# An RWKV-6 recurrence with a feed-forward layer behind it: the v loads of twenty chunks requested by ScalarE's queue instead of SyncE's

## The chip, the cores and the metric

The kernel runs on one core of a Trainium2 chip. The metric is the device time of one execution in microseconds, the median of several runs. A core has five engines that work through a queue of instructions each: TensorE (PE in the profile; its weight loads are PEld), VectorE (DVE), ScalarE (ACT), GpSimd (POOL) and SyncE (SP). Data moves between the memory of the chip (HBM) and the core's on-chip memory by DMA: an engine issues a request, and 16 DMA engines carry it out while the engine goes on. SP computes nothing and does little else than issue requests.

## What is computed

Inputs r, k, v, w have 4 batches, 8 heads, 768 positions and 48 numbers per head, in float32. For each batch and head a 48 x 48 state is carried along the positions; then a feed-forward layer follows.

```
for t in range(S):
    cur = einsum('bhd,bhe->bhde', u * k[t], v[t])
    y[t] = einsum('bhd,bhde->bhe', r[t], state + cur)
    state = w[t][..., None] * state + einsum('bhd,bhe->bhde', k[t], v[t])
x = y as [3072, 384]
h = x @ w_in                 # 384 -> 2048
out = maximum(0.01 * h, h) @ w_out   # 2048 -> 384
```

## The kernel before, in words

**Tiles and stages.** The positions are cut into chunks of 128: 6 chunks for each of 4 batches, 24 in all. Chunks 0 to 3 are worked on two at a time (`pair`, line 487), chunks 4 to 23 are the twenty single chunks (`single`, line 694). For a single chunk:
- Four loads bring w, k, r and v of the chunk (192 KB each, in rows of 192 bytes) into the four quarters of one buffer of the pool "in", which has 11 buffers (lines 705 to 711). All four are requested by SP.
- ACT takes the logarithm of w (line 718), PE sums it along the positions (724), DVE adds (736), ACT takes exponentials (745, 750, 754), DVE multiplies them with r and k into rk (407), and rk is transposed, by PE with copies by ACT or DVE (418, 423, 425) or by a DMA (771).
- POOL casts v to bfloat16, vb (line 457), and makes the bonus term: k times u (437), times r (441), DVE's sum over the head (445), times v into vs (449). POOL also scales the state, sb (782).
- PE multiplies the scores (864), DVE masks them (795). PE then forms the sums k x v for the next state out of rk and vb (line 805), and the chunk's output out of sb (831) and of the masked scores and vb (836). Both need vb. DVE adds vs to the output (482), and it is transposed into xT (468 with 473 or 475, or 849).

The feed-forward layer takes one or two chunks at a time in 14 blocks: PE multiplies xT with w_in (line 1030), ACT applies the leaky maximum while it copies to g (1045), PE multiplies g with w_out (1060). The last seven blocks multiply with seven products instead of eight of the halves (line 960, with sums by DVE at 941 and copies by ACT at 976 and DVE at 981).

**What sets the order.** The kernel first writes down 1124 steps, each with its possible engines and what it depends on (`Plan.add`). The list ORDER (lines 100 to 153) is a fixed sequence of all steps, and FORCE names the engine of a step that has more than one. `Plan.order` walks along ORDER with a model of times: it keeps a clock for each engine, decides from it which buffer of a pool a step gets, and for a load holds the issuing engine back while more than 150 KB would be in flight. The instructions are then written out in ORDER, so every engine's queue is ORDER cut down to the steps of that engine; nothing is reordered on the chip. Real waits are by semaphores: an instruction waits until the data it reads has been written and the buffer it writes is no longer read. Modelled times also decide how many warm-up matmuls (line 1099) are put into PE's early gaps, for planned times under 24 us.

The steps of the twenty v loads are 148, 177, 206, 226, 266, 298, 330, 353, 390, 410, 450, 470, 507, 527, 562, 582, 619, 639, 670, 696, for chunks 4 to 23 in this order. In ORDER the v load stands where its turn in SP's queue comes, among steps of other engines that were planned later in time; for instance

```
... 780, 783, 224, 236, 241, 225, 235, 242, 243, 177, ...   (177: chunk 5's v load; 780: ACT, line 1045)
... 273, 285, 226, ...   (226: chunk 7's v load; 273: ACT, line 750)
... 1029, 639, ...   (639: chunk 21's v load; 1029: ACT, line 976)
```

Of the kernel before, what the change touches and what calls it, by code (L numbers as in the profile page):

```python
# [22 lines left out]
class Plan:  # L23
# [16 lines left out]
    def order(self, pools):  # L40
        left = [len(s[3]) for s in self.steps]
        users = [[] for _ in self.steps]
        for i, s in enumerate(self.steps):
            for j in s[3]:
                users[j].append(i)
        remain, free = {}, {p: [(0.0, k) for k in range(len(t))] for p, t in pools.items()}
        for s in self.steps:
            for b in (*s[4], *s[5]):
                remain[id(b)] = len(b.users)
        n = len(self.steps)  # L50
        self.start, self.done, self.eng, ready = [None] * n, [0.0] * n, [None] * n, [0.0] * n
        at, wire_free, landed, flying = dict(self.BEGIN), 0.0, 0.0, []
        for i in ORDER:
            engs, fn, deps, reads, takes, wire = self.steps[i][0], *self.steps[i][1:2], *self.steps[i][3:]
            if left[i]:
                raise RuntimeError(("before its inputs", i))
            e = FORCE.get(i) or next(iter(engs))
            now = max(at[e], ready[i])
            for b in takes:
                if b.t is None:  # L60
                    slot = min(free[b.pool])
                    free[b.pool].remove(slot)
                    now, b.slot, b.t = max(now, slot[0]), slot[1], pools[b.pool][slot[1]]
            touched = list({id(b): b for b in (*reads, *takes)}.values())
            for b in touched:
                if b.pool == "ps":
                    now = max([now, *(t for q, t in b.seen.items() if q != e)])
            self.start[i], self.eng[i] = now, e
            at[e] = now + engs[e] - (self.OVER[e] if engs[e] > 0.3 else 0.0)
            if wire is None:  # L70
                self.done[i] = now + engs[e] + self.SEEN[e]
            else:
                time, size, lat, lead = wire
                while flying and sum(x for _, x in flying) + size > 150:
                    at[e] = max(at[e], flying.pop(0)[0])
                wire_free = max(wire_free, at[e] + lead) + time
                flying.append((wire_free, size))
                landed = self.done[i] = max(wire_free + lat, landed + 0.7 * time)
            for b in touched:
                b.seen[e] = self.done[i]  # L80
                b.free_at = max(b.free_at, self.done[i])
                remain[id(b)] -= sum(u == i for u in b.users)
                if not remain[id(b)]:
                    free[b.pool].append((b.free_at, b.slot))
            for j in users[i]:
                left[j] -= 1
                ready[j] = max(ready[j], self.done[i])
        if len(set(ORDER)) != n or len(ORDER) != n:
            raise RuntimeError(("order", n, len(ORDER)))
        return ORDER  # L90


LOAD = (1.1, 64, 1.4, 0.2)
# [60 lines left out]
FORCE = {4: "ACT", 6: "DVE", 24: "ACT", 27: "ACT", 30: "DVE", 33: "ACT", 47: "ACT", 57: "ACT", 59: "DVE", 60:  # L154
    "ACT", 62: "DVE", 80: "ACT", 83: "ACT", 86: "DVE", 89: "ACT", 103: "ACT", 113: "DVE", 115: "DVE", 116:
    "DVE", 118: "DVE", 120: "POOL", 122: "POOL", 124: "POOL", 126: "POOL", 128: "ACT", 129: "POOL", 131: "ACT",
    132: "POOL", 134: "DVE", 135: "ACT", 137: "POOL", 138: "POOL", 140: "POOL", 141: "POOL", 143: "POOL", 144:
# [10 lines left out]
def kernel(  # L168
# [11 lines left out]
    nc = tc.nc  # L180
    B, H, S, D = r.shape
    L = 128
# [77 lines left out]
    with tc.manual_schedule():  # L260
# [10 lines left out]
        for t in pools["lw"]:  # L271
# [3 lines left out]
            out=trev[:], in_=trev[:], compare_op=ALU.is_ge, fill=0.0,  # L275
# [5 lines left out]
            out=tstr2[:], in_=tstr2[:], compare_op=ALU.is_gt, fill=0.0,  # L281
# [4 lines left out]
            out=ident[:], in_=ident[:], compare_op=ALU.is_equal, fill=0.0,  # L286
# [3 lines left out]
            out=maskb[:], in_=maskb[:], compare_op=ALU.is_gt, fill=0.0,  # L290
            base=0, pattern=[[1, 128]], channel_multiplier=-1,
        )
        for tile_, op in ((mask2, ALU.is_gt), (spread, ALU.is_equal)):
            for q in (0, 64):
                nc.gpsimd.affine_select(
                    out=tile_[q : q + 64, :, :], in_=tile_[q : q + 64, :, :], compare_op=op, fill=0.0,
# [58 lines left out]
        def columns(n):  # L355
            xb, off = place[n]
            return lambda: xb.t[:, :, off : off + L]
# [23 lines left out]
        for part in (1, 2):  # L381
            def rest(e, part=part):
# [8 lines left out]
                out=u_rows.t[0:1, :], in_=u_row.t[0:1, :]),  # L391
# [302 lines left out]
        def single(n):  # L694
            b, c = seq[n]
            t0 = c * L
            P0 = n * 10
            first, last = c == 0, c == C - 1
            rows[n] = out[b * S + t0 : b * S + t0 + L, :]
            slot = Buf("in")  # L700

            def part(i):
                return lambda: slot.t[:, i * DM : (i + 1) * DM].rearrange("p (h d) -> p h d", h=H)

            lds = []
            for i, src in enumerate((w, k, r, v)):
                def load(e, src=src, i=i):
                    nc.sync.dma_start(out=part(i)(), in_=src[b, :, t0 : t0 + L, :].rearrange("h p d -> p h d"))
                lds.append(step(
                    {"SP": 0.62}, load, P0 + i * 0.1, takes=[slot], wire=LOAD,  # L710
                    deps=[firsts[n - AHEAD]] if n - AHEAD in firsts else []))
            wl, kl, rl, vl = lds
            wv, kv, rv, vv = (part(i) for i in range(4))
# [5 lines left out]
                P0, deps=[wl], reads=[slot], takes=[lw])  # L719
# [3 lines left out]
            def cum(e):  # L723
# [13 lines left out]
                P0, deps=[s_cum], reads=[cp, lw], takes=[ci])  # L737
# [3 lines left out]
            for half in range(0 if first else 2):  # L741
# [4 lines left out]
                        out=a_in.t[q0 : q0 + 64, :, half], in_=cp.t[q0 : q0 + 64, DM : DM + NP], func=AF.Exp),  # L746
                    P0, deps=[s_cum], reads=[cp], takes=[a_in]))
# [3 lines left out]
                P0, deps=[s_cum, s_ci], reads=[cp])  # L751
# [3 lines left out]
                P0, deps=[s_ci], reads=[ci], takes=[ek])  # L755
# [3 lines left out]
                P0, deps=[rl, s_er], reads=[slot, cp], takes=[rk])  # L759
            s_k = step(  # L760
                {"DVE": 0.55}, lambda e: mult(rk.t[:, 1, :, 0:D], heads(ek.t), kv()),
                P0, deps=[kl, s_ek], reads=[slot, ek], takes=[rk])
# [5 lines left out]
            else:  # L768
# [3 lines left out]
                        out=rkT.t[:], in_=rk.t[:].rearrange("p a h d -> p (a h d)")),  # L772
                    P0, deps=[s_r, s_k], reads=[rk], takes=[rkT], wire=TRK)]
# [3 lines left out]
            if not first:  # L777
# [5 lines left out]
                        out=sb.t[:].rearrange("p g a d -> p (g a) d"),  # L783
# [12 lines left out]
                    out=m.t[:, par, :, :], in0=sc[par].t[:].rearrange("p (g t) -> p g t", g=NP),  # L796
# [49 lines left out]
            else:  # L846
# [3 lines left out]
                        out=columns(n)(), in_=y.t[:].rearrange("p h d -> p (h d)")),  # L850
# [4 lines left out]
        def run(ns):  # L855
            works = [single(n) for n in ns]
            asked = [next(x) for x in works]

            def scores(e):
                for sc, rkT, _ in asked:  # L860
                    for p in range(NP):
                        for par in range(2):
                            q0 = 64 * par
                            nc.tensor.matmul(  # L864
                                sc[par].t[:, p * 128 : (p + 1) * 128], lhsT=rkT.t[q0 : q0 + D, NP + p, :],
                                rhs=rkT.t[q0 : q0 + D, p, :], start=True, stop=True, skip_group_check=True)

            s_sc = step(
                {"PE": 0.19 + 0.231 * len(ns)}, scores, ns[-1] * 10 + 1, deps=[s for x in asked for s in x[2]],
                reads=[x[1] for x in asked], takes=[b for x in asked for b in x[0]])  # L870
            given.append(s_sc)
            for x in works:
                next(x, None)
# [142 lines left out]
        for nb, size in enumerate(blocks):  # L1016
# [7 lines left out]
            for j in range(0, NJ, J):  # L1024
# [15 lines left out]
                if j == 0:  # L1040
                    for ch in chs:
# [4 lines left out]
                        out=g.t[:, j : j + J, 0:N],  # L1046
                        in_=hp.t[:, 0 : J * N].rearrange("p (a n) -> p a n", a=J), func=AF.Prelu, alpha=0.01),
# [86 lines left out]
```

## Time and profile before

| | |
|---|---|
| runs before | 179.13 us median of 3 (179.12 to 180.2) |
| span of the profiled execution, first to last instruction | 177.0 us |
| median of the runs less this span | 2.1 us |
| ACT's DMA requests in the profile | 1 (u, 1.5 KB) |
| SP's loads of w, k, r, v for single chunks | 80, of 192 KB each |
| busy share of PE, DVE, ACT, POOL | 96, 81, 64, 61% |

The profile gives no time of its own for the profiled execution beside the span; 2.1 us is taken for what lies around it. A row of the timeline has the start in us, the length in us, the engine and line, what is written and read, how many instructions are merged into the row, and in brackets how long the engine sat idle before it and what ended that. Rows of a DMA request (SPq, ACTq) tell how long the issuing queue was held, not how long the data took. A row of the view by stretches has, after its bounds, its length and then the busy times of PE, PEld, DVE, ACT and POOL with the number of instructions, the granted clock, the DMA share and GB/s. A row of a line's view has its number of instructions with the shortest, median and longest duration in ns. A row of the waits has the total in us, the number of waits, and the longest.

### The profile page before, as it was taken

How to read it: one execution, taken by the hardware profiler on the slowest of the kernel's cores; microseconds unless marked ns; L12 is line 12 of the kernel's file. 1: busy time of each engine (PE TensorE's matmuls, PEld its weight loads, DVE VectorE, ACT ScalarE, POOL GpSimd, SP SyncE). 2: the span in 40 equal slices, each digit the busy share in tenths (PEclk: the TensorE clock that was granted, in tenths of full speed). 3: DMA queues.
4: the chain of work that ended last, by engine and by line, in shares of the span. 5: the costliest groups of instructions: out<-in, count | busy, mean ns of one | idle time of the engine just before them, and what ended most of it. 6: DMA issues, size and time to landing. Idle time of an engine off the chain costs nothing.

```text
span 177.0 us, 5530 instructions
## 1 busy us (share of the span) xinstructions
PE 170.4 (96%) x2155; PEld 139.9 (79%) x2158; DVE 143.5 (81%) x299; ACT 114.0 (64%) x263; POOL 107.3 (61%) x143
## 2 busy tenths in 40 slices
PE   7999999999999999999999999999999998999993
PEld 2566779867768877777779899899899997799992
DVE  7498935267599899889879999999999999956662
ACT  5676769734677794796379964676769950178500
POOL 5989946486749859879599093391693959100000
PEclk9999999999999999999999999999999999999999
DMA  5999999999999999999999999996999897432104
GB/s 138 261 271 340 350 300 195 351 231 199 201 206 195 191 199 227 163 201 179 198 206 195 197 208 209 163 222 124 210 194 196 188 226 78 118 101 80 44 26 157
DMA packets 115885, 34.25 MB, mean 194 GB/s; under 512 B 108305, under 2 KB 115090, under 8 KB 115858
## 3 DMA queue, kind: packets, MB, share of 16 engines
q1 hardware_dynamic: 115856, 33.89, 93.1%
q8 instruction: 17, 0.28, 0.7%
q14 instruction: 10, 0.08, 0.2%
q10 hardware_dynamic: 2, 0.00, 0.0%
HBM read 25.17 MB, written 4.72 MB: 169 GB/s over the span
## 4 chain that ended last, share of the span: by engine, by line
PE 69%; DVE 15%; ACT 5%; issue 4%; DMA 3%; POOL 2%; DVEq 0%; SPq 0%; ACTq 0%
PE ps L1030 30%; PE ps L1060 13%; PE ps L960 10%; DVE rk L407 3%; DMA rkT<-rk 3%; PE ps L864 3%; DVE in L941 2%; PE ps L418 2%; ACT g L425 2%; PE ps L724 1%; PE ps L836 1%; DVE ci L736 1%; PE ps L518 1%; DVE dg L445 1%; ACT ps L750 1%
## 5 line engine op out<-in xcount | busy, mean ns | idle before, releaser
L1030 PE MATMUL ps<-xT,w_in_b 128*128 128x256 bf16 (+1 forms) x672 | 70.8, 258 | 0.3 <-DVE rk L407 0.2
L1045 ACT ACTIVATE g<-ps 128x512 bf16<-128x512 f32 x96 | 54.4, 598 | 18.1 <-PE ps L1030 16.0
L1030 PEld LDWEIGHTS <-w_in_b 128*128 128x128 bf16 x672 | 56.9, 98 | 7.8 <-issue 0.6
L437 POOL TENSOR_TENSOR ru<-in,ub 128x384 f32<-128x384 f32 x24 | 24.3, 1017 | 13.1 <-DMA in<-in_k_dram 7.0
L1060 PE MATMUL ps<-w_out_b,g 128*128 128x384 bf16 x160 | 31.4, 326 | 0.0
L407 DVE TENSOR_TENSOR rk<-in,ps 128x384 bf16<-128x384 f32 x48 | 24.8, 547 | 6.1 <-ACT ps L754 2.3
L782 POOL TENSOR_TENSOR sb<-s,a 128x384 bf16<-128x384 f32 x18 | 15.6, 875 | 16.6 <-ACT a L745 8.1
L795 DVE TENSOR_TENSOR m<-ps,maskb 128x512 bf16<-128x512 f32 x40 | 25.1, 682 | 0.3 <-PE ps L864 0.2
L441 POOL TENSOR_TENSOR ru<-ru,in 128x384 f32<-128x384 f32 x24 | 23.8, 1000 | 2.1 <-DMA in<-in_r_dram 1.1
L1060 PEld LDWEIGHTS <-g 128*128 128x128 bf16 x160 | 14.1, 97 | 6.8
L449 POOL TENSOR_TENSOR vs<-in,dg 128x384 f32<-128x384 f32 x20 | 17.4, 874 | 3.0 <-DMA in<-in_v_dram 2.1
L960 PEld LDWEIGHTS <-g 128*128 128x128 bf16 x224 | 18.3, 98 | 0.2
L976 ACT COPY o<-ps 128x192 f32<-128x192 f32 x18 | 5.8, 320 | 17.5 <-PE ps L960 15.5
L960 PEld LDWEIGHTS <-in 128*128 128x128 bf16 x168 | 13.6, 98 | 1.9 <-DVE in L941 1.4
L445 DVE TENSOR_REDUCE dg<-ru 128x8 f32<-128x384 f32 x24 | 12.9, 545 | 1.9 <-POOL ru L441 1.7
L457 POOL CAST vb<-in 128x384 bf16<-128x384 f32 x24 | 12.7, 534 | 2.2 <-DMA in<-in_v_dram 2.2
L981 DVE TENSOR_TENSOR o<-ps,o 128x192 f32<-128x192 f32 x35 | 11.6, 351 | 1.9 <-ACT o L976 1.1
L482 DVE TENSOR_TENSOR y<-ps,vs 128x384 bf16<-128x384 f32 x20 | 10.9, 553 | 2.4 <-PE ps L836 2.3
L754 ACT ACTIVATE ps<-ci 128x384 f32<-128x384 f32 x20 | 9.8, 493 | 4.7 <-DVE ci L736 4.1
L718 ACT ACTIVATE lw<-in 128x384 bf16<-128x384 f32 x20 | 9.9, 521 | 4.1 <-DMA in<-in_w_dram 4.1
L736 DVE TENSOR_TENSOR ci<-ps,lw 128x384 f32<-128x384 f32 x20 | 10.9, 551 | 1.8 <-PE ps L724 1.1
L960 PE MATMUL ps<-in,in 128*128 128x192 bf16 x112 | 11.4, 247 | 0.5 <-DVE in L941 0.5
(105 smaller groups left out, 258.8 us busy)
## 6 DMA issues: line engine op xcount, KB each, us to landing
out_dram<-o SPq DMA_DIRECT2D x23, 192.0 KB, 2.8
in<-in_w_dram SPq DMA_DIRECT2D x20, 192.0 KB, 4.7
in<-in_k_dram SPq DMA_DIRECT2D x20, 192.0 KB, 4.2
in<-in_r_dram SPq DMA_DIRECT2D x20, 192.0 KB, 4.2
in<-in_v_dram SPq DMA_DIRECT2D x20, 192.0 KB, 4.1
in<-in_moe_w_out_dram SPq DMA_DIRECT2D x4, 768.0 KB, 6.9
in<-in_moe_w_in_dram SPq DMA_DIRECT2D x2, 768.0 KB, 9.7
in<-in_moe_w_in_dram SPq DMA_DIRECT2D x4, 384.0 KB, 8.1
```

The lines of the kernel that those rows point to most:

```text
L407: (nc.gpsimd if e == "POOL" else nc.vector).tensor_tensor(out=o, in0=x, in1=i, op=ALU.mult)
L437: lambda e: nc.gpsimd.tensor_tensor(out=ru.t[:], in0=kv(), in1=ubv, op=ALU.mult),
L441: lambda e: nc.gpsimd.tensor_tensor(out=ru.t[:], in0=ru.t[:], in1=rv(), op=ALU.mult),
L445: lambda e: nc.vector.tensor_reduce(out=dg.t[:], in_=ru.t[:], axis=AX.X, op=ALU.add),
L449: lambda e: nc.gpsimd.tensor_tensor(out=vs.t[:], in0=vv(), in1=dg.t[:].unsqueeze(2).to_broadcast([128, H, D]), op=ALU.mult),
L457: {"POOL": 0.56}, lambda e: nc.gpsimd.tensor_copy(out=vb.t[:], in_=vv()),
L782: lambda e: nc.gpsimd.tensor_tensor(out=sb.t[:].rearrange("p g a d -> p (g a) d"), in0=s_in.t[:].rearrange("p g a d -> p (g a) d"), in1=a_ ...
L795: lambda e, par=par: nc.vector.tensor_tensor(out=m.t[:, par, :, :], in0=sc[par].t[:].rearrange("p (g t) -> p g t", g=NP), in1=maskb[:].uns ...
L960: nc.tensor.matmul(o(), lhsT=x()[:, i, :], rhs=y()[:, i, :], start=fresh, stop=(stop and i == ii[-1]), skip_group_check=True)
L1030: nc.tensor.matmul(hp.t[:, a * N : (a + 1) * N], lhsT=w_in_b[:, t, (j + a) * 128 : (j + a + 1) * 128], rhs=xb.t[:, t, 0:N], start=(a == 0 ...
L1045: lambda e, hp=hp, g=g, j=j, J=J, N=N: nc.scalar.activation(out=g.t[:, j : j + J, 0:N], in_=hp.t[:, 0 : J * N].rearrange("p (a n) -> p a n ...
L1060: nc.tensor.matmul(op.t[:, 0:DM], lhsT=g.t[:, j, off : off + 128], rhs=w_out_b[:, j, :], start=(j == 0), stop=(j == NJ - 1))
```

## The change

The twenty v load steps get ACT as a second possible engine, and FORCE sends all twenty to it; ORDER stays as it is. So the request is written into ACT's queue at the place where the step stands in ORDER. In the model, the data in flight is counted for SP and ACT apart, and a request takes 0.1 us of ACT.

```diff
-        at, wire_free, landed, flying = dict(self.BEGIN), 0.0, 0.0, []
+        at, wire_free, landed, flying = dict(self.BEGIN), 0.0, 0.0, {"SP": [], "ACT": []}
...
-                while flying and sum(x for _, x in flying) + size > 150:
-                    at[e] = max(at[e], flying.pop(0)[0])
+                out = flying[e]
+                while out and sum(x for _, x in out) + size > 150:
+                    at[e] = max(at[e], out.pop(0)[0])
                 wire_free = max(wire_free, at[e] + lead) + time
-                flying.append((wire_free, size))
+                out.append((wire_free, size))
...
+FORCE = {148: "ACT", 177: "ACT", 206: "ACT", 226: "ACT", 266: "ACT", 298: "ACT", 330: "ACT", 353: "ACT", 390: "ACT", 410: "ACT", 450: "ACT", 470: "ACT", 507: "ACT", 527: "ACT", 562: "ACT", 582: "ACT", 619: "ACT", 639: "ACT", 670: "ACT", 696: "ACT",
...
-                    nc.sync.dma_start(out=part(i)(), in_=src[b, :, t0 : t0 + L, :].rearrange("h p d -> p h d"))
+                    (nc.scalar if e == "ACT" else nc.sync).dma_start(
+                        out=part(i)(), in_=src[b, :, t0 : t0 + L, :].rearrange("h p d -> p h d"))
                 lds.append(step(
-                    {"SP": 0.62}, load, P0 + i * 0.1, takes=[slot], wire=LOAD,
+                    {"SP": 0.62, "ACT": 0.1}, load, P0 + i * 0.1, takes=[slot], wire=LOAD,
```

The loads of w, k and r, the transposes by DMA, the weights and the stores stay on SP.

More of the change, by code (lines that the diff above doesn't have):

```diff
@@ L153 @@
     1115, 1116, 1112, 1113, 1119, 1117, 1118, 1121]
-FORCE = {4: "ACT", 6: "DVE", 24: "ACT", 27: "ACT", 30: "DVE", 33: "ACT", 47: "ACT", 57: "ACT", 59: "DVE", 60:
+FORCE = {148: "ACT", 177: "ACT", 206: "ACT", 226: "ACT", 266: "ACT", 298: "ACT", 330: "ACT", 353: "ACT", 390: "ACT", 410: "ACT", 450: "ACT", 470: "ACT", 507: "ACT", 527: "ACT", 562: "ACT", 582: "ACT", 619: "ACT", 639: "ACT", 670: "ACT", 696: "ACT",
+    4: "ACT", 6: "DVE", 24: "ACT", 27: "ACT", 30: "DVE", 33: "ACT", 47: "ACT", 57: "ACT", 59: "DVE", 60:
     "ACT", 62: "DVE", 80: "ACT", 83: "ACT", 86: "DVE", 89: "ACT", 103: "ACT", 113: "DVE", 115: "DVE", 116:
```

## The prediction

> **What bounds the kernel now.** I read the page first (busy times, the chain that ended last, the costliest groups), then the engines' busy time by stretch, then the requests of the loads, and last the timelines of SP, ACT, POOL and PE around the v loads.
>
> ```profile
> span 177.0 us, 5530 instructions
> PE 170.4 (96%) x2155; PEld 139.9 (79%) x2158; DVE 143.5 (81%) x299; ACT 114.0 (64%) x263; POOL 107.3 (61%) x143
> PE 69%; DVE 15%; ACT 5%; issue 4%; DMA 3%; POOL 2%; DVEq 0%; SPq 0%; ACTq 0%
> ```
> ```profile
> 36.00:58.00 22.00, 21.69 (x280) 16.06 (x276) 17.65 (x36) 13.23 (x32) 16.14 (x22) 1.00 1.13 207
> 58.00:84.00 26.00, 26.00 (x293) 20.09 (x290) 23.91 (x46) 19.71 (x47) 21.59 (x25) 1.00 1.11 193
> 84.00:110.00 26.00, 26.00 (x348) 22.58 (x347) 23.03 (x45) 17.72 (x45) 16.62 (x22) 1.00 1.04 203
> 110.00:140.00 30.00, 29.94 (x386) 27.09 (x384) 28.91 (x60) 22.65 (x60) 17.63 (x21) 1.00 0.98 185
> 140.00:158.00 18.00, 17.04 (x233) 15.22 (x232) 16.89 (x33) 6.97 (x17) 9.12 (x12) 1.00 0.71 132
> ```
>
> PE is busy for 170.4 of 177.0 us; between 36 and 158 us, where the single chunks are worked on, it rests 0.31 + 0.00 + 0.00 + 0.06 + 0.96 = 1.3 us of 122. The granted clock is 1.00 throughout. Every engine takes its work in a written order, and PE has no spare time in it: whatever makes one matmul of this stretch wait makes the end that much later, unless a later wait absorbs it. A gain, on the other hand, can hardly exceed that 1.3 us.
>
> **What is moved.** Twenty requests of v leave SP's queue and enter ScalarE's, at the same places of the order list.
>
> ```profile
> L708 SPq DMA_DIRECT2D in<-in_v_dram x20: 368/679/2054, 30.1 to 144.8; - x20
> DMA to landing us min/median/max: 3.1/4.2/7.2
> ```
> ```profile
> in<-in_v_dram SPq DMA_DIRECT2D x20, 192.0 KB, 4.1
> ```
>
> A request keeps SP for 0.37 to 2.05 us (median 0.68) and the data is there 3.1 to 7.2 us after the request began, for v 4.1 us in the median. SP loses 20 x 0.68 = 13.6 us of work, and the loads of w, k and r behind the old places can go earlier by about 0.7 us each. SP is not on the chain (SPq 0%), so I cost that gain at nothing; what would show if it were worth more is the 1.3 us of PE's rest.
>
> The point that decides is when ScalarE comes to the request. The list was made for SP, which runs ahead: it has nothing to compute, so it asks for v long before its neighbours in the list are run. ScalarE reaches the same place only after the ACT step before it, and that step often waits for PE. The first, second, fourth, seventh and eighteenth of the twenty (chunks 4, 5, 7, 10, 21) are the ones that matter. In the list their requests (148, 177, 226, 330, 639) come behind the ACT steps 183 (line 754), 780 (1045), 273 (750), 358 (745) and 1029 (976). First the old requests of three of them, then the ACT steps, then POOL's work on v, then the matmuls that need it:
>
> ```profile
> 30.10 1.24 SPq L708 DMA_DIRECT2D in<-in_v_dram  x1
> ...
> 44.08 0.85 SPq L708 DMA_DIRECT2D in<-in_v_dram  x1
> ...
> 137.67 0.57 SPq L708 DMA_DIRECT2D in<-in_v_dram  x1
> ```
> ```profile
> 37.01 0.49 ACT L754 ACTIVATE ps<-ci 128x384 f32<-128x384 f32 x1
> ...
> 49.82 0.60 ACT L1045 ACTIVATE g<-ps 128x512 bf16<-128x512 f32 x1
> ...
> 53.90 0.47 ACT L750 ACTIVATE ps<-ps 128x384 f32<-128x384 f32 x1
> ...
> 75.25 0.15 ACT L745 ACTIVATE a<-ps 64x4 f32<-64x4 f32 x1
> ...
> 87.22 0.86 ACT L475 COPY xT<-ps 128x384 bf16<-128x384 bf16 x2 [2.66 <-PE ps L468]
> ...
> 142.84 0.47 ACT L750 ACTIVATE ps<-ps 128x384 f32<-128x384 f32 x1 [0.65 <-DVE ci L736]
> ...
> 144.50 0.32 ACT L976 COPY o<-ps 128x192 f32<-128x192 f32 x1 [0.25 <-PE ps L960]
> ```
> ```profile
> 37.30 0.51 POOL L457 CAST vb<-in 128x384 bf16<-128x384 f32 x1 [0.50 <-DMA in<-in_v_dram]
> ...
> 48.65 0.50 POOL L457 CAST vb<-in 128x384 bf16<-128x384 f32 x1
> ...
> 76.27 0.83 POOL L449 TENSOR_TENSOR vs<-in,dg 128x384 f32<-128x384 f32 x1
> 77.04 0.50 POOL L457 CAST vb<-in 128x384 bf16<-128x384 f32 x1
> ...
> 144.76 0.50 POOL L457 CAST vb<-in 128x384 bf16<-128x384 f32 x1
> ```
> ```profile
> 39.02 0.36 PE L836 MATMUL ps<-vb,m 128*128 128x48 bf16 x8
> ...
> 47.69 0.83 PE L1030 MATMUL ps<-xT,w_in_b 128*128 128x128 bf16 x12
> ...
> 49.20 0.49 PE L836 MATMUL ps<-vb,m 128*128 128x48 bf16 x8
> ...
> 56.66 0.36 PE L836 MATMUL ps<-vb,m 128*128 128x48 bf16 x8
> ...
> 79.44 0.33 PE L805 MATMUL ps<-vb,rk 128*128 128x96 bf16 x4
> ...
> 93.19 0.33 PE L805 MATMUL ps<-vb,rk 128*128 128x96 bf16 x4
> ...
> 145.98 0.37 PE L836 MATMUL ps<-vb,m 128*128 128x48 bf16 x8
> ...
> 147.02 0.36 PE L836 MATMUL ps<-vb,m 128*128 128x48 bf16 x8
> ```
>
> Chunk 5 is the plainest. SP asked for its v at 44.08; ScalarE comes to that place at 49.82, and by then POOL has cast it (48.65) and PE has begun to multiply with it (49.20). The data cannot be there in time, whatever the queue does.
>
> **Two unknown prices.** Does a request wait until the ACT instruction before it ends, or only until it has begun? The one request on ACT so far (u's) stands first on its queue and cannot tell. The bounds are the begin and the end, 0.15 to 0.6 us apart by the rows above; I take the begin and 0.05 us. How long until v lands from a queue of its own? At least the 3.1 us of the quickest load; the 4.1 us median holds loads that lay behind SP's earlier ones, and v would no longer; against that it shares the 16 engines with SP's loads. I take the middle, 3.6 us, and keep 3.1 and 4.2 for the range.
>
> **The sum**, request + 3.6 us + the cast's 0.50, against the time at which PE wants it:
> - chunk 4: 37.06 + 4.1 = 41.2 against 39.02: 2.1 us
> - chunk 5: 49.87 + 4.1 = 54.0 against 49.20: 4.8 us
> - chunk 7: 53.95 + 4.1 = 58.05 against 56.66: 1.4 us
> - chunk 10, where the product of line 449 (0.77 us to the next start) goes ahead of the cast: 75.30 + 3.6 + 0.77 + 0.50 = 80.2 against 79.44: 0.7 us
> - chunk 21: 144.55 + 4.1 = 148.65 against 145.98: 2.7 us
>
> Together 11.7 us. The other fifteen cost nothing in this sum. The nearest of them are chunks 12 and 13, both asked for behind the second copy of line 475 (which begins halfway through its row, near 87.6): 91.2, then cast, product and cast (0.50 + 0.77 + 0.50) give 93.0 against 93.19; and chunk 20: 142.89 + 4.1 = 147.0 against 147.02. With 4.2 us these two cost up to 0.6 us each.
>
> Two corrections. While PE waits for chunk 4, ScalarE catches up: the step ahead of chunk 5's request needs only the matmuls of 47.69 to 48.52, and could run some 1.1 us before 49.82. I take 0.5 us off; the floor is 0, the end 1.1. And each request holds ACT for some time: 20 x 0.37 to 0.68 is 7 to 14 us on an engine with 63 us idle. What of it delays PE no row shows. It is between nothing (a hold cannot hasten ACT) and 13.6 us; most falls into ACT's waits for PE, and I take 1 us. POOL is an in-order engine too: behind the late cast wait the products k*u and r of the next chunk and, behind them, DVE's reduce of line 445. While PE is held as long as POOL, that costs nothing more; I leave it to the range. The edits of the planning model (a limit on the data in flight for each queue instead of one for all) change only its reckoned times, and with them which buffer a step gets; the warm-up matmuls, which hang on reckoned times under 24 us, lie ahead of the first request (30.10), so I cost this at nothing; if a step gets a buffer that comes free later, that is a wait of some tenths more or less. The late load itself adds no wait for a free buffer, since w of the same chunk has asked for the buffer before.
>
> 11.7 - 0.5 + 1.0 = 12.2 us. The profiled span of 177.0 us lies 2.1 us under the median of 179.13 us; with the same 2.1 us around it, 177.0 + 12.2 + 2.1 = **191.3 us**.
>
> **The rivals.**
> 1. *Only the unavoidable part.* ScalarE and DVE catch up at each stop of PE, and v lands in 3.1 us. Then chunks 4, 5, 7 and 21 cost 1.6, 4.3, 0.9 and 2.2 us, less some 1.1, 0.5 and 1.1 of catching up at the last three: 6.3 us, 185.4 us. For it: DVE and ACT have time to catch up as soon as PE stands. Against it: ACT's steps ahead of chunks 7 and 21 follow PE or DVE closely, so that there is little to catch up.
> 2. *The request's own hold becomes the cost.* If a request on ACT lasts as on SP, and waits for SP's current one as well (up to 2 x 0.68 us), ScalarE loses 27 us in the stretch where it is busy 66 to 76% (19.71 of 26.00, 22.65 of 30.00), and a third of it reaches PE: about 9 us on top, 200 us. Against it: the ACT idle time is mostly waits for PE, in which a hold is free. The Trainium skill (Perfetto Trace Analysis, DMA Instruction — HWDGE) counts a wait for the lock of a shared generator into such a request; no run here shows a request on ACT beside a busy SP.
> 3. *Not slower: SP was the narrow place.* SP is relieved of 13.6 us, w, k and r land sooner, v has a queue of its own, and the 1.3 us of PE's rest go: 177.8 us. It decides only if ScalarE comes to each request some 4.1 us before the matmul. In the sum it does so for fifteen chunks and not for five; for chunk 5 it comes after the matmul. The Trainium skill (DMA: Bandwidth & Descriptors, Issuing engines are not separate DMA queues) says that a second issuing engine saves only the sequencer's issue time, since the same 16 engines move all data. By that rule alone the time would stay at 179.1 us; it says nothing of when the new issuer reaches its request, and the rows for chunk 5 speak against no change.
>
> **How the numbers follow.** My forecast 0.75, rival 1 0.10, rival 2 0.10, rival 3 0.05. The low end is rival 1's 185; the high end takes 4.2 us for the landing, the end of the ACT step as the start and 4 us for holds: 5 chunks x about 1.0 us more, chunks 12 to 20 about 2 us, holds 3 us more, 10 us over the forecast, rounded up to 202. About 1% is what a measurement of this kernel can tell from no change. Faster by over 1%: 0.02; within 1%: 0.03; slower: 0.95.
>
> **What would show it.** Before, POOL waited for v so long:
>
> ```profile
> POOL vb L457 <- DMA in<-in_v_dram: 2.2, 4, 0.9
> POOL vs L449 <- DMA in<-in_v_dram: 2.1, 1, 2.1
> ```
>
> In the changed profile these two should be 10 us and more together, and PE line 836 waiting for that cast, longest at chunk 5, near 51 us. The v requests should stand under ACTq, each right behind the ACT step named. POOL and PE busy times stay as they are. I am wrong if PE's idle time between 36 and 158 us grows by less than 4 us, if PE waits for ACT rather than for POOL, or if v lands in under 2 us or over 5 us.

## The result, and the profile after

The changed kernel takes 201.7 us (median of three runs, 199.9 to 202.5 us) against 179.1 us (179.7 us with a fourth run of the kernel before): a ratio of 1.1235 with a 95% interval of 1.115 to 1.132, some 22 us more. Here and below a time is the median of the runs within 1.5% of the fastest of the same kernel, as the ratios are taken from those. The direction and the mechanism of the forecast held; its 191.3 us caught a little over half of the loss. The profile below comes from an execution of 204.6 us (span 202.9 us), so its sums are some 3 us above the middle. The change moves lines behind the planner down by 2 or 3: 836 is now 839, 457 is 459, 708 is 710.

The page, the busy times first, then the groups of POOL's cast and of PE's product with it (the idle time before them is behind the bar), and the v loads' issues:

```profile
span 202.9 us, 5527 instructions
PE 174.8 (86%) x2155; PEld 142.4 (70%) x2158; DVE 144.5 (71%) x299; ACT 115.0 (57%) x263; POOL 109.1 (54%) x143
L459 POOL CAST vb<-in 128x384 bf16<-128x384 f32 x24 | 12.7, 536 | 38.5 <-DMA in<-in_v_dram 38.5
L839 PE MATMUL ps<-vb,m 128*128 128x48 bf16 x160 | 7.5, 186 | 18.8 <-POOL vb L459 18.8
in<-in_v_dram ACTq DMA_DIRECT2D x20, 192.0 KB, 4.8
```

No engine but PE works noticeably longer. POOL waits 38.5 us for v where it waited 2.2, and PE waits 18.8 us for POOL's casts where it waited for none. The view of the request's line has how long the requests hold ACT and when their data is there (the second row takes all loads of the line together):

```profile
L710 ACTq DMA_DIRECT2D in<-in_v_dram x20: 374/376/2012, 36.0 to 169.4; - x20
DMA to landing us min/median/max: 2.9/5.1/8.4
```

PE's timeline: every stop of more than 0.5 us in the stretch of the single chunks is here.

```profile
44.91 0.48 PE L839 MATMUL ps<-vb,m 128*128 128x48 bf16 x8 [6.36 <-POOL vb L459]
61.73 0.48 PE L839 MATMUL ps<-vb,m 128*128 128x48 bf16 x8 [5.53 <-POOL vb L459]
72.87 0.36 PE L839 MATMUL ps<-vb,m 128*128 128x48 bf16 x8 [2.25 <-POOL vb L459]
109.00 0.32 PE L727 MATMUL ps<-lw,trev 128*128 128x384 bf16 x1 [1.67 <-ACT lw L721]
153.55 0.36 PE L839 MATMUL ps<-vb,m 128*128 128x48 bf16 x8 [2.45 <-POOL vb L459]
172.03 0.36 PE L839 MATMUL ps<-vb,m 128*128 128x48 bf16 x8 [2.20 <-POOL vb L459]
```

The stop at 109.00 is before the sum of a w load's logarithm; the others belong to chunks 4, 5, 7, 18 and 21. Five stops before products with v make 18.8 us. The span grew by 25.9 us: 18.8 for these, 1.7 for the stop at 109.00, 174.8 - 170.4 = 4.4 us of longer busy time because PE was slower in places, and 1.0 in small pieces. Where it was slower the view by stretches tells (the sixth number behind the length is the granted clock), here around the stop of chunk 4:

```profile
38.50:41.40 2.90, 0.05 (x1) 0.00 (x0) 0.43 (x1) 0.53 (x1) 0.00 (x0) 1.00 1.23 279
41.40:44.80 3.40, 0.00 (x0) 0.00 (x0) 0.00 (x0) 0.00 (x0) 0.45 (x1) 0.51 0.91 138
44.80:48.30 3.50, 3.39 (x25) 2.02 (x25) 2.08 (x5) 0.34 (x2) 3.19 (x5) 0.50 0.78 154
48.30:51.70 3.40, 3.40 (x47) 2.81 (x46) 2.16 (x6) 2.73 (x6) 3.32 (x5) 1.00 0.00 0
```

PE stands from 38.5, the clock halves at 41.4 and comes back at 48.3, and in the 3.5 us after the stop PE gets 25 matmuls done where the next 3.4 us hold 47.

### The profile page after: what moved, and what is told of

It reads as the page before. It is cut to its first block, busy times and chain, and to the rows that moved or that the text cites. A ratio compares the mean times of both kernels' runs of the same rounds, so it can differ in the third digit from the quotient of the medians.

```text
span 202.9 us, 5527 instructions
## 1 busy us (share of the span) xinstructions
PE 174.8 (86%) x2155; PEld 142.4 (70%) x2158; DVE 144.5 (71%) x299; ACT 115.0 (57%) x263; POOL 109.1 (54%) x143
## 5 line engine op out<-in xcount | busy, mean ns | idle before, releaser
L1033 PE MATMUL ps<-xT,w_in_b 128*128 128x256 bf16 (+1 forms) x672 | 71.6, 259 | 0.3 <-DVE s L823 0.2
L1063 PE MATMUL ps<-w_out_b,g 128*128 128x384 bf16 x160 | 33.7, 343 | 0.0
L459 POOL CAST vb<-in 128x384 bf16<-128x384 f32 x24 | 12.7, 536 | 38.5 <-DMA in<-in_v_dram 38.5
L839 PE MATMUL ps<-vb,m 128*128 128x48 bf16 x160 | 7.5, 186 | 18.8 <-POOL vb L459 18.8
L785 POOL TENSOR_TENSOR sb<-s,a 128x384 bf16<-128x384 f32 x18 | 16.4, 916 | 12.0 <-DVE s L823 5.2
L1063 PEld LDWEIGHTS <-g 128*128 128x128 bf16 x160 | 14.8, 102 | 7.8 <-issue 1.5
L451 POOL TENSOR_TENSOR vs<-in,dg 128x384 f32<-128x384 f32 x20 | 18.6, 934 | 3.0 <-DMA in<-in_v_dram 1.7
L839 PEld LDWEIGHTS <-m 128*128 128x128 bf16 x160 | 6.3, 98 | 19.5 <-issue 19.5
L963 PEld LDWEIGHTS <-g 128*128 128x128 bf16 x224 | 18.3, 98 | 0.2
L963 PEld LDWEIGHTS <-in 128*128 128x128 bf16 x168 | 14.1, 100 | 1.9 <-DVE in L944 1.3
L984 DVE TENSOR_TENSOR o<-ps,o 128x192 f32<-128x192 f32 x35 | 11.7, 352 | 2.7 <-ACT o L979 1.9
```

Source lines behind the costliest of these rows:

```text
L451: lambda e: nc.gpsimd.tensor_tensor(out=vs.t[:], in0=vv(), in1=dg.t[:].unsqueeze(2).to_broadcast([128, H, D]), op=ALU.mult),
L459: {"POOL": 0.56}, lambda e: nc.gpsimd.tensor_copy(out=vb.t[:], in_=vv()),
L785: lambda e: nc.gpsimd.tensor_tensor(out=sb.t[:].rearrange("p g a d -> p (g a) d"), in0=s_in.t[:].rearrange("p g a d -> p (g a) d"), in1=a_ ...
L839: nc.tensor.matmul(yp.t[:, h * D : (h + 1) * D], lhsT=m.t[:, h % 2, h // 2, :], rhs=vb.t[:, h, :], start=(first and h == 0), stop=(h == H ...
L963: nc.tensor.matmul(o(), lhsT=x()[:, i, :], rhs=y()[:, i, :], start=fresh, stop=(stop and i == ii[-1]), skip_group_check=True)
L1033: nc.tensor.matmul(hp.t[:, a * N : (a + 1) * N], lhsT=w_in_b[:, t, (j + a) * 128 : (j + a + 1) * 128], rhs=xb.t[:, t, 0:N], start=(a == 0 ...
```

## The experiments

Theory P is the forecast's: ScalarE comes late to its request, so v is late and PE stands. Its rivals are H (the request holds ScalarE) and Q (two queues on the same 16 DMA engines lengthen all loads). All ratios are to the kernel before on the same chip.

**The same queue, earlier places.** All twenty requests stay on ScalarE and only move in the list; in the code, behind FORCE:

```diff
+EARLY = {148: 748, 177: 214, 206: 759, 226: 759, 266: 790, 298: 796, 330: 814, ...}
+for _v, _a in EARLY.items():
+    ORDER.remove(_v)
+    ORDER.insert(ORDER.index(_a) + 1, _v)
```

> The changed kernel with the twenty v requests still on ScalarE, but each moved forward in the order list, behind the ScalarE step that ran about 1.5 us before SP made the same request in the kernel before. Theory P (the place in ScalarE's order makes v late, and PE stands): v is asked for as early as before, so PE's waits at line 839's matmuls go and with them the half clock; 179 to 181 us. Theory H (a request's hold of ScalarE, 20 x 0.4 us and more, is the cost): the holds are all still there, 195 us or more. Theory Q (two queues on the same 16 DMA engines lengthen every load, and that is the cost): also still there, 190 us or more.

Measured: 180.1 us, ratio 1.0053 (1.0022 to 1.0084). 96% of the loss (1 - 0.0053 / 0.1235) is gone, with ScalarE's queue, its twenty requests and the edit of the planning model unchanged. The profile is from a run of the same kernel by itself:

> The kernel with the twenty requests some 1.5 us ahead of SP's old time once more, for a look at its profile at full clock. Theory P: 179 to 181 us, no wait of PE before the products with v, and POOL's waits for v at 1 to 5 us in all.

Measured: 180.5 us in one execution, with this row of the waits, these two of the request's line (the second again for all its loads), and PE's longest stop past the start:

```profile
POOL vb L464 <- DMA in<-in_v_dram: 2.0, 3, 1.4
```
```profile
L715 ACTq DMA_DIRECT2D in<-in_v_dram x20: 373/375/622, 27.2 to 144.1; - x20
DMA to landing us min/median/max: 3.3/5.0/7.5
```
```profile
49.61 0.36 PE L844 MATMUL ps<-vb,m 128*128 128x48 bf16 x8 [0.73 <-DVE rk L414]
```

No stop of over 0.5 us was ended by POOL's cast. The holds are still there, 8.2 us in all where the changed kernel has 10.4; the longest is 0.6 us instead of 2.0. What Q starts from is there as well: the loads of the line land after 5.0 us in the median, 5.1 in the changed kernel and 4.2 before. But with the requests early enough that costs next to nothing. Moving the requests forward by 4 us instead of 1.5 gained nothing more:

> The twenty v requests on ScalarE, moved forward still further: behind the ScalarE step that ran about 4 us before SP made the same request. Theory P: once v is early enough, more changes nothing; 179 to 180.5 us, and a look at whether relieving SP's queue of 20 loads gains anything (rival 3 would have 177.8). If the earlier requests take the DMA engines from loads that are needed sooner: 181 us or more.

Measured: 181.1 us, 1.0099 (1.0065 to 1.0133), a little above P's 180.5 us and at the 181 us expected if early requests take the DMA engines from loads that are needed sooner; this was not tested further. So taking twenty loads from SP is worth nothing here, and no version of the change beat the kernel before.

**Which requests.** FORCE is cut down, so that the other v loads go back to SP:

```diff
+for _v in [206, 266, 298, 330, 353, 390, 410, 450, 470, 507, 527, 582, 619, 670, 696]:
+    del FORCE[_v]
```

> The changed kernel with only the v requests of chunks 4, 5, 7, 18 and 21 on ScalarE, those before whose matmuls PE stood in its profile; the other fifteen are back on SP. Theory P: nearly the whole loss stays, 18.8 us of waits and about 5 us of half clock less what varies; 196 to 202 us. Theories H and Q: a quarter of the requests, so a quarter of the 22 us; 184 to 187 us.

Measured: 198.8 us, 1.1054 (1.0971 to 1.1137). Five requests carry 19 of the 22 us, as P has it and H and Q have not. PE stood at chunks 4, 5, 7 and 21; chunk 18's v landed 4.9 us after its request instead of 7.2, and there was no stop.

```profile
44.39 0.48 PE L842 MATMUL ps<-vb,m 128*128 128x48 bf16 x8 [5.70 <-POOL vb L462]
59.91 0.48 PE L842 MATMUL ps<-vb,m 128*128 128x48 bf16 x8 [3.85 <-POOL vb L462]
71.67 0.36 PE L842 MATMUL ps<-vb,m 128*128 128x48 bf16 x8 [1.95 <-POOL vb L462]
166.16 0.36 PE L842 MATMUL ps<-vb,m 128*128 128x48 bf16 x8 [2.72 <-POOL vb L462]
```

> The complement: the v requests of chunks 4, 5, 7, 18 and 21 are back on SP, the other fifteen stay on ScalarE at the late places. Theory P: near the kernel before, 179 to 183 us, with perhaps one new short wait where the cover was thin (chunks 10, 12, 13, 20). Theories H and Q: three quarters of the 22 us, 193 to 197 us.

Measured: 185.4, 185.9, 188.8 and 190.0 us; the lower two give 185.6 us, some 6 us above the kernel before. That is a miss for P as I had put it, and for H and Q as well. The profile (185.9 us) shows two byways of which my forecast had left the first to the range. POOL and PE around chunks 20 and 21:

```profile
150.32 0.50 POOL L462 CAST vb<-in 128x384 bf16<-128x384 f32 x1 [5.10 <-DMA in<-in_v_dram]
150.79 0.83 POOL L454 TENSOR_TENSOR vs<-in,dg 128x384 f32<-128x384 f32 x1
151.57 0.83 POOL L788 TENSOR_TENSOR sb<-s,a 128x384 bf16<-128x384 f32 x1
152.34 0.50 POOL L462 CAST vb<-in 128x384 bf16<-128x384 f32 x1
```
```profile
152.90 0.36 PE L842 MATMUL ps<-vb,m 128*128 128x48 bf16 x8 [2.37 <-POOL vb L462]
```

Chunk 21's v, on SP, had landed at 147.59; but POOL works in order and stood 5.1 us before chunk 20's cast, so chunk 21's cast came at 152.34 and PE lost 2.4 us on it. The same happened with 0.8 us at chunk 7 behind chunk 6. The second byway is ScalarE's own row of requests for chunks 12 to 15, the same in the changed kernel:

```profile
103.94 0.38 ACTq L710 DMA_DIRECT2D in<-in_v_dram  x1
104.06 0.48 ACT L477 COPY xT<-ps 128x384 bf16<-128x384 bf16 x1
104.36 0.59 ACTq L710 DMA_DIRECT2D in<-in_v_dram  x1
105.89 0.60 ACT L1048 ACTIVATE g<-ps 128x512 bf16<-128x512 f32 x1 [1.35 <-PE ps L1033]
105.96 2.43 ACTq L710 DMA_DIRECT2D in<-in_v_dram  x2
108.43 0.52 ACT L721 ACTIVATE lw<-in 128x384 bf16<-128x384 f32 x1 [1.94 <-DMA in<-in_w_dram]
```

The last row says that the logarithm waited for w. But SP's w load of that chunk, by the trace, had landed at 106.71; what ended at 108.39 was the fourth request (105.96 + 2.43), the longest hold of all (2012 ns). So ScalarE was held itself while three v loads of its queue were in flight, and PE lost 1.67 us at 109.00 (1.83 us at 94.13 in the run with fifteen). Only at this bunch is H seen at work. A third stop of the run with fifteen, 1.66 us at 41.49, belongs to neither byway and comes up again below. Leaving out chunks 6, 20 and 12 to 15 as well tests both byways at once:

> The changed kernel with only the v requests of chunks 8, 9, 10, 11, 16, 17, 19, 22 and 23 on ScalarE. Left out against the run with fifteen: chunks 6 and 20 (POOL stood before their casts and so came late to the casts of chunks 7 and 21) and chunks 12 to 15 (asked for in one bunch, after which a load of w came late). Theory P with these two byways: none of them is left, 179 to 181 us. If any late request costs by its number: 9 of 15 of that run's 6.5 us, 183 us or more; theories H and Q: 9 of 20 of 22 us, 189 us.

Measured: 181.6 us, 1.0135 (1.0101 to 1.017), a little above P's 181. The profile has no stop of PE for v over 0.5 us. It has one of 1.5 us near 41.7, before the sum of chunk 6's logarithm; that stop is also in the profile of the next experiment, where v is on SP throughout, and not in the profile of before. It follows chunk 6's load of w: before, SP asked for it at 34.78 and it was there at 39.40; in the run with nine it was asked for at 35.27 and there at 41.10. Why it takes 5.8 us there instead of 4.6 stays open. A shorter stop, 0.8 us at 139.33, waited for the logarithm of another w load.

**The hold alone.** The kernel before, with a small request by ScalarE at each of the twenty places:

```diff
+    tiny = pool.tile([128, DM], F32, name="tiny")
...
                 def load(e, src=src, i=i):
                     nc.sync.dma_start(out=part(i)(), in_=src[b, :, t0 : t0 + L, :].rearrange("h p d -> p h d"))
+                    if i == 3:
+                        nc.scalar.dma_start(out=tiny[n : n + 1, :], in_=u.rearrange("h d -> (h d)").unsqueeze(0))
```

> The kernel before, all loads on SP, with twenty requests more: at each of the twenty places of the changed kernel ScalarE requests 1.5 KB of u into a row of a tile that nothing reads. So ScalarE is held twenty times, and v isn't late. Theory P: the holds fall into ScalarE's idle time; 179 to 181 us. Theory H (the hold costs): 20 x 0.4 us reach PE; 185 us or more.

Measured: 180.0 us, 1.0047 (1.0015 to 1.0079).

```profile
L711 ACTq DMA_DIRECT2D tiny<-in_u_dram x20: 208/209/507, 36.5 to 146.3; - x20
```

Each request held ACT's queue for some 0.21 us, a little over half of a full load's 0.38. The stop near 41 us (1.45 us) is in this profile too, so the 0.8 us need not be the holds'. The early places have twenty full holds, 8.2 us in all, at a ratio of 1.0053. H doesn't carry the loss.

**The clock.** Matmuls of zeros keep PE busy while it would stand; they add work that the result doesn't use.

```diff
             def intra(e):
+                for _ in range({4: 26, 5: 22}.get(n, 0)):
+                    nc.tensor.matmul(yp.t[:], lhsT=zeros[:, 0:128], rhs=zeros[:], start=True, stop=True,
+                                     skip_group_check=True)
```

> The changed kernel with 26 and 22 matmuls of zeros (512 columns each, about 0.21 us) written into the result's bank ahead of the products of chunk 4 and chunk 5, where PE stood for 6.4 and 5.5 us; the products start afresh after them, and they wait for nothing but the bank. Theory C (PE's clock falls to half because it stands still, and the slow start after it is a cost of its own): the clock stays at 1.00 around both stops, and 3 to 3.5 us of the loss come back; 198 us where the changed kernel has 201.7. If the clock falls for another reason, or is no cost: no change, 201 to 202 us, or more by the added matmuls.

Measured: 200.9 us, 1.1184 (1.1056 to 1.1312), against 201.7 us, 1.1235 (1.115 to 1.132): no difference that could be told. The clock did stay at 1.00 from 36 to 60 us, and chunk 7's request came 3.7 us earlier (64.07 instead of 67.77 us); but then chunk 7's stop was longer and had its own stretch of half clock, as had the stops at 107.95 and 169.13.

```profile
70.05 0.36 PE L842 MATMUL ps<-vb,m 128*128 128x48 bf16 x8 [3.12 <-POOL vb L459]
```

What was gained early was lost again later, if it was a gain. A kernel with one stop is cleaner: chunk 5 alone on ScalarE, without and with the added matmuls, in two turns.

> The kernel with the v request of chunk 5 alone on ScalarE, the chunk whose request comes after the old time of its matmul. Theory P: one stop of PE of 4 to 5.5 us before line 836's matmuls (by this kernel's numbering), then a stretch of 3.4 us at half clock (1.7 us): 184.5 to 186.5 us. Without a cost of the clock 183 to 184.5. Theories H and Q: a twentieth of the loss, 180 to 181 us.

> The same, chunk 5 alone on ScalarE, with 22 matmuls of zeros of 512 columns (4.7 us) ahead of chunk 5's product, so that PE doesn't stand. Theory C (the half clock after a stop is a cost of its own): the clock stays at 1.00, and the time is 1.2 to 1.8 us under the run without them. If it is no cost: the same time or longer.

> Chunk 5 alone on ScalarE, with 18 matmuls of zeros (3.9 us) instead of 22, which ended 0.4 us after the cast. Theory C: clock at 1.00, and 1.0 to 1.6 us under the run without them that is measured beside it. If the half clock costs the end nothing: the same time.

> Chunk 5 alone on ScalarE without added matmuls, again, beside the run with 18 of them on the same chip: 185 to 186.5 us, as before.

Measured: chunk 5 alone 186.0 us, 1.0376 (1.0338 to 1.0415), and again 185.9, 1.0394 (1.0346 to 1.0442). One request of twenty costs some 7 us: in the profile a stop of 4.2 us, the slow start after it, and 1.5 us of that stop near 41 us. With 22 matmuls 185.6, 1.0362 (1.0324 to 1.04), not the 1.2 to 1.8 us less that theory C (a cost of the half clock of its own) expected; they ended 0.4 us after the cast. With 18 it is 184.8, 1.0341 (1.0304 to 1.0378), 0.9 us (by the ratios) to 1.1 us (by the medians) under the run beside it, near the lower edge of what C expected. The stop and what follows, first without, then with the 18:

```profile
54.17 0.48 PE L842 MATMUL ps<-vb,m 128*128 128x48 bf16 x8 [4.19 <-POOL vb L462]
...
57.94 0.33 PE L730 MATMUL ps<-lw,trev 128*128 128x384 bf16 x1
```
```profile
55.43 0.36 PE L845 MATMUL ps<-vb,m 128*128 128x48 bf16 x8 [2.07 <-POOL vb L462]
...
57.71 0.33 PE L730 MATMUL ps<-lw,trev 128*128 128x384 bf16 x1
```

PE still stands for 2.1 us behind the matmuls of zeros, since v took 5.5 us to land in this run and 4.1 in the other, but the clock stayed at 1.00. The same matmuls take 57.94 - 54.17 = 3.8 us after the stop, and 57.71 - 55.43 = 2.3 us where the clock was kept up: the slow start costs 1.5 us. The intervals of the two ratios overlap, and the stop near 41 us differs too (1.4 to 1.5 us without, 0.7 with the 18), so in the whole time that cost is likely and not proved; in the stretch it is seen.

## Why the prediction was right in kind and short in size

**Late places: right.** Four of the five stops for v are at chunks that the sum named, chunk 4's request came at 36.00 us where the sum had 37.06, and moving the requests forward removed 96% of the loss. Chunk 10, 0.7 us in the sum, cost nothing: its v landed in 3.0 us.

**The landing: mis-sized.** "I take the middle, 3.6 us, and keep 3.1 and 4.2 for the range" was the step that failed. Chunk 4's v landed 8.3 us after its request, chunk 5's 5.4, chunk 18's 7.2, and the median of the twenty is 4.8. Chunk 4's stop was 6.4 us instead of 2.1, and chunk 18, which my sum had no cost for, 2.45. For chunk 4 the rows that I quoted told as much: SP's own request began at 30.10, and the cast waited for its data until 37.30, 7.2 us, in the stretch where the weights are loaded. I took one figure for the whole kernel, below the median of 4.1, for transfers in a busy part. That a queue of its own lets a load pass the others was wrong for chunks 4 and 18. By the landings in the trace, chunk 4's v, asked for at 36.00, was there at 44.30, between SP's loads of k (35.63, there at 44.04) and w (36.37, there at 44.77); chunk 18's v, asked for at 145.73, was there at 152.94, and SP's load of k, asked for at 145.75, at 152.61. Where no load of SP's was under way, v landed in 2.9 to 3.0 us (chunks 20 and 21). This agrees with the Trainium skill (DMA: Bandwidth & Descriptors, Issuing engines are not separate DMA queues), in which DMAs of all issuers run on the same 16 engines and interleave. For the waits on v the sum had 11.7 us, and 18.8 were measured.

**The clock: left out.** My sum had waits and holds only. The stops at chunks 4, 5 and 18 each brought a stretch at half clock, with 10.4 us of PE's busy time in them, which is where the 4.4 us of longer busy time lie; the row of one clock of 1.00 before spoke only for a PE that never stands.

**Holds: near in the sum, by luck.** I took 1 us for twenty even holds of 0.4 to 0.7 us. In the changed kernel one hold, 2.0 us for the fourth request of a bunch, cost 1.7, and for the other nineteen no cost is seen; the twenty small requests cost 0.8 us, the stop near 41 us included.

**Begin or end of the ACT instruction: neither.** Chunk 5's request began at 55.68, half a microsecond ahead of the instruction before it in the list:

```profile
55.68 0.44 ACTq L710 DMA_DIRECT2D in<-in_v_dram  x1
55.81 0.48 ACT L1076 COPY o<-ps 128x384 f32<-128x384 f32 x1
56.19 0.60 ACT L1048 ACTIVATE g<-ps 128x512 bf16<-128x512 f32 x1
```

**POOL's order: left to the range.** A late v stops POOL too, and the next chunk's cast with it. Hidden in the changed kernel by the larger stops, it cost 2.4 us by itself in the run with fifteen.

**The range and the signs.** That 201.7 us lies inside the range, just under its end of 202, is luck: the upper end was built of a landing of 4.2 us, 4 us of holds and chunks 12 to 20, and what filled it were landings of up to 8.3 us and the clock. Of the signs, POOL waited for v, and PE for POOL, as said. PE's busy time didn't stay as it was, the longest stop was at chunk 4 and not at 5, and of the 19 landings of v that the trace has, 9 took over 5 us, the bound that I had set for being wrong. The 0.5 us of catching up can't be read off by itself.

**Rivals.** 1 would have needed 3.1 us of landing at chunks 4, 5, 7 and 21, which had 8.3, 5.4, 4.5 and 3.0. 2 holds in one place only, at 109.00. 3 is out: with v in time on its own queue, 1.0053 and 1.0099.

## What to carry to other kernels

The place of a request in a queue is a time only together with what that engine does before it: one that runs ahead, as SP, asks early from the same place in a list where a computing engine asks late. Price a moved load by when the new engine comes there and by the landing time of loads in that very stretch, not by a median. And a stop of PE, where PE bounds the kernel, can cost more than its length when the clock falls behind it: 1.5 us more after chunk 5's.

## What the runs showed of the hardware

In these traces the clock changes at the bounds of windows of 3.4 us with a fixed phase in each run: in the changed kernel it falls at 41.4, 58.5 and 154.1, distances of 5 and 28 windows. A window needs not be idle for the clock to fall in the next. In the run with five requests a stop of 1.95 us was enough:

```profile
69.00:72.40 3.40, 1.45 (x29) 1.21 (x27) 0.55 (x1) 0.78 (x3) 1.28 (x3) 1.00 1.37 184
72.40:75.80 3.40, 3.40 (x24) 2.28 (x22) 2.96 (x7) 1.65 (x5) 3.40 (x5) 0.50 1.13 224
```

while in the changed kernel a stop of 2.25 us, lying across two windows, was not:

```profile
68.70:72.10 3.40, 1.93 (x41) 1.82 (x39) 1.85 (x4) 1.79 (x4) 0.57 (x1) 1.00 1.25 204
72.10:75.50 3.40, 2.63 (x39) 2.04 (x39) 1.85 (x5) 1.14 (x4) 3.18 (x5) 1.00 1.06 219
```

With PE busy for 1.45 us of a window the next one ran at half clock, with 1.93 us it did not. The nearest in the traces are 1.5 us, with half clock behind it (chunk 5 alone with 22 matmuls, the window from 38.65), and 1.6 us, without (the run with fifteen, from 90.70). The Trainium skill (TensorE: Matmul & The Clock Gate, Part 1: The HAM clock gate) has the free-running window of 3.4 us, which the traces bear out; it has the clock fall after an idle window, and here a window that was two fifths busy was enough.
